# A windowed attention and MLP kernel: masks in three operations, the first loads in two portions, and a new hand-written order of all engines

## The chip, the cores and the metric

The kernel runs on one core of one Trainium2 chip. The metric is device time in microseconds (us) of one execution. The core has five engines that run their own instruction streams and meet only at semaphores: TensorE (PE in the profile; PEld is its weight load), VectorE (DVE), ScalarE (ACT), GpSimd (POOL) and SyncE (SP), which here issues nearly all DMA transfers.

## The reference, cut to what matters

There are 4 batches, 8 heads, 768 positions and a head size of 64. A query sees the `n_local` = 96 positions up to itself and the first `n_global` = 8 positions of the sequence; both numbers arrive as inputs. The bias falls with the distance, by a slope for each head. Behind attention stands an MLP from 512 to 2048 and back, on all 3072 rows.

```python
rel = pos[:, None] - pos[None, :]
is_global = pos[None, :] < int(n_global)
is_local = (rel >= 0) & (rel < int(n_local))
keep = is_global | is_local
dist = np.where(is_global & ~is_local, float(n_local), np.abs(rel))
scores = np.where(keep, scale * q @ k.T - slopes[:, None, None] * dist, -1e9)
a = softmax(scores); x = (a @ v).reshape(B * S, H * D)
h = x @ w_in                                   # 512 -> 2048
out = (h * tanh(log1p(exp(h)))) @ w_out        # 2048 -> 512
```

## The kernel before, in words

The work is cut into 12 chunks of 256 query rows (`NC`), three to a batch. A chunk has 16 attention pairs of a head and a 128-row block, taken in 8 tiles of two heads each; a tile sees its own 128 keys and, but for a sequence's first block, 104 more (96 before it and 8 global ones), so its score block is 128 or 232 columns wide. The MLP of a chunk has 8 steps of two 128-wide slices of the hidden layer.

`windowed` (L115) holds one small function for each step and, at its end, the table `PROGRAM`. Each word of the table is one call: a letter for the function (the dictionary `acts`) and a number for the tile, load, weight block or step; a stroke behind it (`L1'`) gives a copy to DVE instead of ACT, or a subtraction to DVE instead of POOL. Under `manual_schedule` every engine runs its instructions in just this order, and so do the transfers in SP's queue. Nothing reorders them: a wait on one engine holds back all that stands behind it there.

The words that matter here, with the lines of the profile:

- `e` (`begin`, L305): matmuls on a tile of ones (L313) whose result nothing reads; they only keep PE at work.
- `I`, `K0`, `K1` (L263 to L281): on DVE, the identity and the distances `d0` (own 128 columns) and `rel` (all 232), with a huge value where a key is not seen. They need `n`, which is loaded as 64-bit words and put together by L69 to L71. `L` and `M` scale them into the bias of each head, `mb0` and `mb` (a copy, L150 on DVE and L152 on ACT).
- `s` (`scores`, L426): for two tiles, the matmuls of q and k. `t` (`largest`, L440): on DVE, scores plus bias, and the row maximum. `y` (`exps`, L449): the exponentials on ACT. `P` (`turn_p`, L479): transposes on PE, `F` copies them out of PSUM (L150 or L152). `W` (`weigh`, L502 or L507): the product with v.
- The first three chunks (`CF32`) run in 32-bit matmuls straight on what was loaded; the others split every operand into two 16-bit halves.
- `q`, `v`, `x`, `w` (`load_qk` L165, `load_v`, `window_v`, `load_w` L325): loads. One `w` block is 512 KB. The weights come as 64-bit floats and are converted by `A`, `S`, `B` (`bits_w`, L364), `C` (L368), `D`, `E`.
- `i` (`moe_in`, L570) and `o` (`moe_out`, L626): the two matmuls of an MLP step; `j u n r` (ACT) and `G H` (DVE) are the activation between them, `z Z` its split into two halves.
- `Q` (`evacuate`, L628) and `Y` (`store`): results out of PSUM, and to memory. For the last chunk, `evacuate` takes each 128-row tile in two halves of 256 columns, the first on ACT (L635), the second on DVE (L636), and one store on SP follows (L642).
- `f` (`flags`, L646): four one-element operations on DVE that test `n`; only the last check needs them.

Of the kernel before, what the change touches and what calls it, by code (L numbers as in the profile page):

```python
# [42 lines left out]
def tile_kernel(ctx, tc, qd, kd, qT, kT, v, n, w_in, w_out, out):  # L43
# [71 lines left out]
def windowed(st, tc, loc):  # L115
# [49 lines left out]
    def load_qk(G):  # L165
        if G >= 2 * NC:
            return
        ci, g = divmod(G, 2)
        b, c = divmod(ci, NCHB)
        o = OWN if c == 0 else 0  # L170
        pairs = slice(g * GH // 2, (g + 1) * GH // 2)
        qr = raws.tile([P, GH // 2, CH], F32, name="qr", bufs=3)
        kr = raws.tile([P, GH // 2, KW], F32, name="kr", bufs=3)
        nc.sync.dma_start(qr, L.qT[b].rearrange("(a j) d s -> (j d) a s", j=2)[:, pairs, c * CH:(c + 1) * CH])
        for j in range(2):
            half = slice(j * D, (j + 1) * D)
            (nc.scalar if G == 0 and j else nc.sync).dma_start(kr[half, :, o:], L.kd[ci, half].rearrange("p (a j) w -> p a j w", j=2)[:, pairs, j, o:])
        raw[G] = (qr, kr)
# [71 lines left out]
    FAR = 2.0 ** 39  # L250
    jj = mt.tile([P, P], F32, name="u", bufs=3)
# [365 lines left out]
    def moe_out(m):  # L617
        ci, fp = divmod(m, NFP)
        if fp == 0:
            pos[ci] = [ps.tile([P, DM], F32, name=f"{'pav' if ci == 1 else 'po'}{t}", bufs=1) for t in range(2)]  # L620
        gt = gts.pop(m)
        for t in range(2):
            for j in range(2):
                fb = 2 * fp + j
                for n, (x, y) in enumerate(((0, 0), (0, 1), (1, 0))):
                    nc.tensor.matmul(pos[ci][t], gt[:, x, j, t * P:(t + 1) * P], wv4[:, 2 * fb + 1, y, :], start=(fb == 0 and n == 0), stop=(fb == NFB - 1 and n == 2))  # L626
# [19 lines left out]
    def flags():  # L646
        nc.vector.tensor_scalar(fl[:, 0:1], L.n_f[0:1, 0:1], 0.0, None, op0=ALU.is_ge)
# [15 lines left out]
    def checks(i):  # L663
# [40 lines left out]
        R2 H0 P17 s18 O2 W15 W14 y16 A4 F17 z0 t19 y19 C7 t18 T2' U2 E3 E1 Z0 P16 s20 P19 C4 t20 B6 t21 y18 F19 y20 F16' D4' E4' S5' A5 B12 R3 B5 o0 P20 P18
        s22 y21 F20 S12 A12 W17 O3 S6 T3 F18 A6 A8 C5 D7' t22 U3 W19 W20 P21 i8 E7 B8 C6 C12 t23 S8' D6' y22 F21 y23 j8 D5 E6 G8 E5' C8 B13 B10 S13' W21 P23
        W18 W16 P22 F22' R4 F23 u8 n8 S10 D12 r8 A13 D8 W23 i1 i9 w16 w11 E12 E8 H8 j1 A10 u1 S9 z8' C13 G1 j9 O4 W22 A14' Z8' C10 D10' R5 o8 u9 n1 n9 r1 r9
        T4 A15 S14 A11 E10 G9 A9' D13' E13 H1 U4 B14 i2 i10 z1 B9 C14 B15 B11 H9 Z1 S11 j2 z9 C11 C9 G2 h3' Z9' j10 u10 n10 D9 D11 r10 D14 u2 n2 S15' G10
        E9' S16' C15 H10 z10' r2 D15 A16 E14 w18 w24 w22 w21 w20 w17 w25 q6 w19 w26 Z10 H2 E11' o1 o9 i3 o10 O5 B16 S18 C16 A18 z2 j3 E15 Z2 u3 A17 n3 T5
        S17 A20 S20' r3 D16' G3 A24 B18 B17 U5 E16' B20 C18 B24 C17 D17 H3 o2 i11 i16 j11 z3 S24 G11 D18' E18 i12 w28 q7 w23 u11 J16 A22 n11 r11 Z3 C20 D20
        j12 A25' B19 E17 H11 S22' G12 A19 z11 C24 Z11' o3 i4 i17 D24 B22 E24 C22 E20 S19 u12 j4 D22 u4 n4 c7 n12 G4 S25' C19 B25 a7' C25 d7' b7 o11 s24 i18  # L710
        D19 r12 J17 r4 E22' H4 N0 t24 D25' A26' H12 t25 z4' J18 y25 A21 z12 E25' l3 E19' Z12' S26' B21 B26 Z4' i13 s26 i5 o12 j13 y24 G13 u13 S21 j5 A28 o4
        i20 q9 w30 w27 S28' C21 C26 D26' E26' B23 B28 t26 A30 u5 n5 D21 C28 g25 r5 n13 B30 G5 J20' S30' g24 E21' y26 r13 A23 H5 S23' i19 i6 p25' z5 A27 C23
        J19' D23 E23' c8' C30 H13 j6 u6 D28 g26 z13 B27 p26' Z5 Z13' D30' G6 E28' E30 p24 d8 w29 X25 w31 v4 X24 q8 x3 X26 i14 o5 i21 j14 u14 n6 r6 n14 S27
        r14 G14 H6 t27 S31 a8 i7 C27 y27 J21 z6 j7 u7 D27 B29 b8 S29' E27 Z6' H14 z14 Z14 i15 s28 o13 o14 o6 n7 r7 j15 u15 a9 n15 A31' A29' B31 G7 H7 t28
        C29 C31 G15 D31' z7' Z7' r15 D29 j16 u16 j17 y28 u17 n17 n16 r16 g27 H15 g28' p28' G16 z15' t29 E29 E31 H16 Z15 z16' G17 p27' Z16' o7 s30 o15 j18
        u18 y29 Q0 r17 q10 X28 Y0 o16 t30 g29' b9 H17 z17' Z17' h4' a11' t31 p29 y30 n18 r18 j19 u19 c9 G18 H18 d9' G19 z18' Z18 n19 Q1 r19 H19 j21 j20 o17
        W24 W25 i22 W26 W28 s32 o18 X29 X27 u21 z19 n21 r21 u20 g30 y31 n20 g31 p30 l4 c10' Z19' G21 t32 G20 t33 H21 p31' v5 x4 X30 X31 o19 W29 i23 W27 s34
        W30 W31 y32 z21 j22 u22 r20 y33 j23 a10 u23 n23 r23 n22 r22 R6 T6' H20 z20' U6 Z21 Z20 G22 g32' R7 T7' U7 H22 b10 z22 Z22' t35 y35 g33 p32' g35'
        d10' c11' d11 p33 G23 H23 t34 p35' o20 o21 V6 V7 o22 i24 s36 i25 Y1 X32 X33 X35 q11 t37 z23' j24 y34 u24 n24 y37 Z23' G24 j25 r24 H24 G25 t36 u25
# [196 lines left out]
```

## Time and profile before

| what | value |
|---|---|
| median of 3 runs | 621.35 us (617.2 to 621.35) |
| the profiled execution's own time | 624.25 us |
| its span, first to last instruction | 622.5 us |
| mean granted TensorE clock | 0.987 |
| PE busy | 610.3 us (98%) |
| DVE busy | 458.1 us (74%) |
| ACT busy | 441.3 us (71%) |
| POOL busy | 157.4 us (25%) |

The profile page cuts the span into 40 slices of 15.6 us; the row PEclk gives TensorE's granted clock in tenths of full speed. The view by windows gives the busy time of each engine in a stretch, the granted clock, the busy share of the DMA engines and what they moved. The timeline gives single instructions with their start, their duration, and in brackets how long the engine had been idle before and what ended that. The chain of waits follows what ended last back to its cause. A busy PE is not yet a PE at its peak, since the ends of matmuls are modelled.

### The profile page before, as it was taken

The numbers are of one execution on the slowest core, as the hardware profiler recorded it, in microseconds if no ns is written. First come the engines' busy times: TensorE is split into PE (matmuls) and PEld (weight loads), VectorE is DVE, ScalarE is ACT, GpSimd is POOL, SyncE is SP. The second block draws the span as 40 slices with busy tenths as digits, with TensorE's granted clock in tenths as the row PEclk, the third lists the DMA queues.
The fourth block names the chain that finished last, engine by engine and source line by source line (L and its number), as shares of the span: only waits on it lengthen the run. The fifth ranks groups of instructions, "written<-read, shape, count | busy, mean of one in ns | idle before, by whom it ended". The sixth has DMA issues, their size and how long they took to land.

```text
span 622.5 us, 13595 instructions
## 1 busy us (share of the span) xinstructions
PE 610.3 (98%) x5081; PEld 423.0 (68%) x5081; DVE 458.1 (74%) x1204; ACT 441.3 (71%) x1106; POOL 157.4 (25%) x130
## 2 busy tenths in 40 slices
PE   7999999999999999999999999999999999999996
PEld 3888867776466767676776676766667766766662
DVE  6599999989998779867676777776785766462443
ACT  5699887779895767766876758866865865665651
POOL 0031343104232250223233203223123332301020
PEclk9699999999999999999999999999999999999999
DMA  8994484235165739317256555392275434310001
GB/s 210 282 294 159 136 271 133 59 126 128 43 139 138 150 72 226 76 26 169 47 116 160 109 134 102 67 200 44 68 165 86 59 68 107 85 35 1 35 1 37
DMA packets 122358, 71.06 MB, mean 114 GB/s; under 512 B 91536, under 2 KB 112016, under 8 KB 122288
## 3 DMA queue, kind: packets, MB, share of 16 engines
q1 hardware_dynamic: 122144, 70.01, 47.3%
q8 instruction: 41, 0.67, 0.5%
q14 instruction: 29, 0.24, 0.1%
q10 hardware_dynamic: 144, 0.14, 0.1%
HBM read 38.62 MB, written 6.29 MB: 72 GB/s over the span
## 4 chain that ended last, share of the span: by engine, by line
PE 83%; DVE 9%; issue 3%; ACT 2%; DMA 1%; SPq 0%; POOL 0%; DVEq 0%; POOLq 0%
PE ph L570 35%; PE po L626 33%; PE sc L426 5%; PE pav L507 4%; PE pav L502 3%; DVE gf L608 2%; PE po L479 1%; DMA wts<-w_in 1%; DVE gf L604 1%; DVE ws L368 1%; PE pav L626 1%; DVE ws L364 1%; DVE gt L156 1%; DVE gt L150 0%; DVE A L440 0%
## 5 line engine op out<-in xcount | busy, mean ns | idle before, releaser
L570 PE MATMUL ph<-xT,wts 128*128 128x256 f16 x2304 | 263.6, 273 | 0.2 <-POOL wts L156 0.2
L570 PEld LDWEIGHTS <-wts 128*128 128x128 f16 x2304 | 222.8, 98 | 35.3 <-issue 1.7
L626 PE MATMUL po<-wts,gt 128*128 128x512 f16 x1056 | 238.7, 379 | 1.1 <-DVE gt L150 0.7
L626 PEld LDWEIGHTS <-gt 128*128 128x128 f16 x1152 | 110.0, 98 | 127.1 <-issue 2.8
L156 POOL TENSOR_TENSOR gt<-gf,gt 128x512 f16<-128x512 f32 x55 | 67.3, 1224 | 278.5 <-DVE gt L150 148.5
L588 ACT ACTIVATE e<-ph 128x512 f32<-128x512 f32 x90 | 53.1, 590 | 92.1 <-PE ph L570 91.8
L608 DVE CUSTOM_DVE_ANT_0 gf<-gf,u 128x512 f32<-128x512 f32 x96 | 79.7, 830 | 44.1 <-ACT u L600 43.1
L449 ACT ACTIVATE A<-A,nm 128x232 f32<-128x232 f32 (+1 forms) x192 | 88.4, 462 | 30.5 <-DVE nm L440 30.5
L604 DVE SCALAR_TENSOR_TENSOR gf<-e,ph 128x512 f32<-128x512 f32 x90 | 61.1, 682 | 53.2 <-ACT e L588 51.9
L440 DVE CUSTOM_DVE_ANT_0 A<-sc,mb 128x232 f32<-128x232 f32 (+1 forms) x192 | 64.3, 375 | 19.3 <-PE sc L426 16.7
L156 POOL TENSOR_TENSOR hl<-A,hl 128x512 f16<-128x512 f32 (+1 forms) x36 | 44.6, 1246 | 74.8 <-DVE hl L150 31.3
L592 ACT ACTIVATE u<-e 128x512 f32<-128x512 f32 x96 | 59.8, 624 | 1.8
L600 ACT ACTIVATE u<-u 128x512 f32<-128x512 f32 x96 | 59.4, 624 | 1.8
L596 ACT ACTIVATE u<-u 128x512 f32<-128x512 f32 x96 | 59.5, 623 | 1.6
L156 POOL TENSOR_TENSOR wts<-ws,wts 128x512 f16<-128x512 f32 x20 | 26.0, 1304 | 87.1 <-ACT wts L152 53.1
L152 ACT ACTIVATE gt<-gf 128x512 f16<-128x512 f32 x44 | 27.4, 623 | 21.3 <-DVE gmax L608 20.6
L449 ACT ACTIVATION_READ_ACCUMULATOR A<-A,nm 128x1 f32 x192 | 36.2, 188 | 0.0
L507 PEld LDWEIGHTS <-AT 128*128 128x128 f16 (+1 forms) x792 | 29.2, 97 | 6.3 <-issue 1.5
L156 DVE TENSOR_TENSOR hl<-A,hl 128x512 f16<-128x512 f32 (+1 forms) x36 | 29.9, 832 | 2.1 <-ACT hl L152 1.7
L156 DVE TENSOR_TENSOR gt<-gf,gt 128x512 f16<-128x512 f32 x41 | 29.0, 706 | 3.3 <-ACT gt L152 2.9
L507 PE MATMUL pav<-vo,AT 128*128 128x64 f16 x432 | 27.8, 192 | 0.0
L426 PE MATMUL sc<-wc,ws 64*128 64x232 f16 (+1 forms) x432 | 26.4, 254 | 0.3 <-DVE nm L440 0.2
(126 smaller groups left out, 608.5 us busy)
## 6 DMA issues: line engine op xcount, KB each, us to landing
qr<-qT SPq DMA_DIRECT2D x24, 256.0 KB
wts<-w_in SPq DMA_DIRECT2D x12, 512.0 KB
wts<-w_out SPq DMA_DIRECT2D x12, 512.0 KB
kr<-kd SPq DMA_DIRECT2D x32, 184.0 KB
out<-ob SPq DMA_DIRECT2D x11, 512.0 KB
vr<-v SPq DMA_DIRECT2D x9, 512.0 KB
vc<-vo SPq DMA_DIRECT2D x15, 192.0 KB
wr<-w_in SPq DMA_DIRECT2D x4, 512.0 KB
```

The source lines that it names most:

```text
L156: (nc.vector if other else nc.gpsimd).tensor_tensor(out, in_, high, op=ALU.subtract)
L426: nc.tensor.matmul(sc[j][:, a2, 0:w], x[half, a2, rows_], y[half, a2, col0:col0 + w], start=(n == 0), stop=(n == len(terms) - 1))
L440: nc.vector.tensor_tensor_reduce(out=A[:, j, 0:w], in0=sc[j][:, 0:w], in1=m, scale=-1.0 / (UNIT if ci < CF32 else UNIT * SQ), scalar=3.0e3 ...
L449: nc.scalar.activation(A[:, j], A[:, j], AF.Exp, bias=nm[:, h:h + 1], scale=-1.0, accum_out=rs[:, h:h + 1])
L507: nc.tensor.matmul(pav[:, cols], AT[rows_, (x * 2 + j) * nk + kk, :], vs[kk][rows_, y, cols], start=(n == 0), stop=(n == last))
L570: nc.tensor.matmul(ph[:, j, :].rearrange("p (b t) -> p b t", b=2), wv4[:, 2 * fb, x, c * P:(c + 1) * P], xT[:, :, y * NCC + c, :], start=( ...
L592: nc.scalar.activation(u, mish[m]["e"], AF.Square, bias=0.5)
L596: nc.scalar.activation(mish[m]["r"], mish[m]["u"], AF.Ln, bias=0.25 / RS, scale=1.0 / RS)
L600: nc.scalar.activation(r, r, AF.Exp, scale=-1.0)
L604: nc.vector.scalar_tensor_tensor(gf, mish[m]["e"], 0.5, mish[m]["h"], op0=ALU.add, op1=ALU.mult)
L608: nc.vector.tensor_tensor_reduce(out=gf, in0=gf, in1=mish[m]["r"], scale=SG / (SV * SW * RS), scalar=0.0, op0=ALU.mult, op1=ALU.max, accum ...
L626: nc.tensor.matmul(pos[ci][t], gt[:, x, j, t * P:(t + 1) * P], wv4[:, 2 * fb + 1, y, :], start=(fb == 0 and n == 0), stop=(fb == NFB - 1 a ...
```

## The change

It does six things.

1. `n` is no longer put together from its two words before the masks: they use the low word (`n_w`), and the three small operations move to `flags`.
2. The masks of the own block take three operations after `n` (L267 once, L272, L273) in place of five; what does not need `n` stands in `identity`, ahead of it.
3. The first q and k loads are cut into two portions, first the 128 columns that the first score block needs; one of the first k portions is issued by ACT, the rest by SP.
4. The matmuls on ones are 10, 4 and 1 in place of 13 and 2, and stand in other places.
5. In the last MLP step the last tile's matmuls run in two halves of 256 columns; the first half is copied by DVE and stored through SP, the last half is copied by ACT and stored by ACT itself.
6. `PROGRAM` is another order up to its last 160 words; many strokes changed too.

```diff
-    two32 = 4294967296.0
     wv = n_w.rearrange("p (n w) -> p n w", w=2)
-    nc.vector.tensor_scalar(n_neg, wv[:, :, 0], 0.0, two32, op0=ALU.is_lt, op1=ALU.mult)
-    nc.vector.tensor_tensor(n_neg, n_neg, wv[:, :, 0], op=ALU.add)
-    nc.vector.scalar_tensor_tensor(n_f, wv[:, :, 1], two32, n_neg, op0=ALU.mult, op1=ALU.add)
...
+        if G == 0:
+            for cq, ck in ((slice(0, P), slice(o, o + P)), (slice(P, CH), slice(o + P, KW))):
+                nc.sync.dma_start(qr[:, :, cq], qs[:, :, cq])
+                for j in range(2):
+                    (nc.scalar if j == 0 and ck.start == o else nc.sync).dma_start(kr[halves_[j], :, ck], ks[j][:, :, ck])
+        else:
+            nc.sync.dma_start(qr, qs)
...
     def identity(i):
         nc.vector.tensor_scalar(idn, rel[:, own], 0.0, None, op0=ALU.is_equal)
+        nc.vector.tensor_scalar(off[:, own], rel[:, own], 0.0, NEVER, op0=ALU.is_lt, op1=ALU.mult)
+        nc.vector.tensor_tensor(rel[:, own], rel[:, own], off[:, own], op=ALU.add)
 
     def outside(cols):
-        nc.vector.tensor_scalar(off[:, cols], rel[:, cols], 0.0, None, op0=ALU.is_lt)
-        nc.vector.scalar_tensor_tensor(off[:, cols], rel[:, cols], L.nlf, off[:, cols], op0=ALU.is_ge, op1=ALU.max)
+        nc.vector.tensor_scalar(off[:, cols], rel[:, cols], nl, FAR, op0=ALU.is_ge, op1=ALU.mult)
 
     def masks_own():
         outside(own)
-        nc.vector.scalar_tensor_tensor(k0, jj, L.ngf, off[:, own], op0=ALU.is_ge, op1=ALU.mult)
-        nc.vector.scalar_tensor_tensor(d0, rel[:, own], L.nlf, off[:, own], op0=ALU.subtract, op1=ALU.mult)
-        nc.vector.tensor_tensor(d0, rel[:, own], d0, op=ALU.subtract)
-        nc.vector.scalar_tensor_tensor(d0, k0, FAR, d0, op0=ALU.mult, op1=ALU.max)
+        nc.vector.scalar_tensor_tensor(k0, jj, ng, off[:, own], op0=ALU.is_ge, op1=ALU.mult)
+        nc.vector.scalar_tensor_tensor(d0, rel[:, own], nl, k0, op0=ALU.min, op1=ALU.max)
...
         for t in range(2):
-            for j in range(2):
...
+            for cols in parts(m, t):
+                for j in range(2):
+                    fb = 2 * fp + j
+                    for n, (x, y) in enumerate(((0, 0), (0, 1), (1, 0))):
+                        nc.tensor.matmul(pos[ci][t][:, cols], gt[:, x, j, t * P:(t + 1) * P], wv4[:, 2 * fb + 1, y, cols], ...)
+    def parts(m, t):
+        if m < NC * NFP - 1 or t == 0:
+            return (slice(0, DM),)
+        return slice(0, DM // 2), slice(DM // 2, DM)
...
-                half = DM // 2
-                nc.scalar.activation(ob[:, t, 0:half], po[t][:, 0:half], AF.Copy, scale=1.0 / (SG * SW))
-                nc.vector.tensor_scalar(ob[:, t, half:], po[t][:, half:], 1.0 / (SG * SW), None, op0=ALU.mult)
-                store(ci, slice(t, t + 1))
+                for cols in parts(NC * NFP - 1, t):
+                    early, final = t and cols.start == 0, t and cols.stop == DM
+                    copy(ob[:, t, cols], po[t][:, cols], 1.0 / (SG * SW), early)
+                    (nc.scalar if final else nc.sync).dma_start(L.out[n * P:(n + 1) * P, cols], ob[:, t, cols])
...
     PROGRAM = """
-        e13 I0 K0 L2 K1 L4 L0 L3 v0 w2 q1 x0 s0 e2 t1 y1 M3 P1 L1' t0 s2 B2 F1' f0 M0 M2 M1 L5 y0 A2 t3 t2 P0 W1 y3 P3 q2 w0 v1 w1 q3 x1 s4 ...
+        e10 I0 v0 q1 K0 K1 L4' L2 x0 s0 e4 L0' L1' L5' L3 M1 t0 t1 y0 L6 M2 q2 s2 y1 L7' M0' M3' P0 t3 w0 P1 F1' F0 y3 w2 e1 W0 t2 M6' W1 y2 P3 f0 s4 ...
```

What the table does to SP's queue at the start (`n_i` is n, `qr` and `kr` are q and k, `vo` is v, `wts` a weight block): before it read

```order
L62 DMA n_i<-n 128x4
L174 DMA qr<-qT 128x2x256
L177 DMA kr<-kd 64x2x264
L211 DMA vo<-v 128x2x512
L333 DMA wts<-w_in 128x4x256
L174 DMA qr<-qT 128x2x256
L177 DMA kr<-kd 64x2x264 x2
```

and now

```order
L62 DMA n_i<-n 128x4
L175 DMA qr<-qT 128x2x128
L177 DMA kr<-kd 64x2x128
L175 DMA qr<-qT 128x2x128
L177 DMA kr<-kd 64x2x136 x2
L215 DMA vo<-v 128x2x512
L179 DMA qr<-qT 128x2x256
L181 DMA kr<-kd 64x2x264 x2
```

The weight block no longer stands ahead of the second group's q and k; the first group's load has become five entries here instead of two.

On DVE, between the maxima of the first two tiles and those of the next two (`A,nm<-sc,mb` 128x232; `ws` and `fl` are a weight conversion and the flags, `AT` a transposed tile), the order was

```order
L440 ISA nm_171 128x1
L364 TENSOR_SCALAR ws<-wts 128x512
L150 TENSOR_SCALAR AT<-po_178 128x256
L647 TENSOR_SCALAR fl<-n_f 1x1
L648 TENSOR_SCALAR fl<-n_f,fl 1x1
L649 TENSOR_SCALAR fl<-n_f,fl 1x1
L650 TENSOR_SCALAR fl<-n_f,fl 1x1
L440 ISA A,nm_208<-sc,mb 128x232
```

and is now

```order
L445 ISA nm_170 128x1
L146 TENSOR_SCALAR mb_95<-u 128x128
L146 TENSOR_SCALAR mb<-e 128x232 x2
L445 ISA A,nm_201<-sc,mb 128x232
L445 ISA nm_201 128x1
L445 ISA A,nm_201<-sc,mb 128x232
```

The weight conversion, which waits for its load, and the flags have left this place; three bias copies have come in.

## Rows read from the trace of the kernel before

**Rows 1.** The profile page: the span, and TensorE's granted clock in 40 slices.

```profile
span 622.5 us, 13595 instructions
...
PEclk9699999999999999999999999999999999999999
```

**Rows 2.** Windows: stretch, its length, busy us by engine (instructions), clock, DMA share, GB/s.

```profile
4.00:6.00 2.00, 2.00 (x7) 0.71 (x6) 1.72 (x7) 0.00 (x0) 0.00 (x0) 1.00 1.04 269
...
8.00:10.00 2.00, 1.64 (x10) 0.96 (x10) 0.46 (x5) 2.00 (x10) 0.00 (x0) 1.00 1.13 293
...
12.00:14.00 2.00, 1.14 (x6) 0.63 (x6) 2.00 (x13) 1.77 (x8) 0.00 (x0) 0.63 1.09 189
14.00:26.00 12.00, 12.00 (x58) 10.00 (x58) 5.60 (x24) 5.23 (x21) 0.00 (x0) 0.50 1.08 274
26.00:28.00 2.00, 2.00 (x19) 2.00 (x19) 1.94 (x11) 1.53 (x5) 0.00 (x0) 0.95 1.08 350
28.00:62.00 34.00, 34.00 (x286) 28.97 (x286) 31.71 (x111) 32.46 (x94) 7.38 (x6) 1.00 0.80 229
62.00:200.00 138.00, 135.77 (x1062) 93.67 (x1060) 129.57 (x281) 113.03 (x260) 41.05 (x31) 1.00 0.46 128
```

**Rows 3.** The chain of waits, first 30 us: start us, us, what.

```profile
3.10 7.23 DMA wts<-w_in
...
17.84 1.85 PE sc L426 x8
...
28.37 0.98 PE sc L426 x8
```

**Rows 4.** Timeline of DVE, 3 to 13 us: start, us, instruction, idle before it.

```profile
3.97 0.17 DVE L69 TENSOR_SCALAR n_neg<-n_w 128x2 f32<-128x2 f32 x1
...
4.57 0.35 DVE L268 SCALAR_TENSOR_TENSOR e<-e,n_f 128x128 f32<-128x128 f32 x1
...
7.40 0.28 DVE L440 CUSTOM_DVE_ANT_0 A<-sc,mb 128x128 f32<-128x128 f32 x1
...
7.82 0.22 DVE L150 TENSOR_SCALAR mb<-u 128x128 bf16<-128x128 f32 x1
...
10.35 0.46 DVE L364 TENSOR_SCALAR ws<-wts 128x512 uint16<-128x512 uint16 x1 [1.89 <-DMA wts<-w_in]
...
11.03 0.13 DVE L647 TENSOR_SCALAR fl<-n_f 1x1 f32<-1x1 f32 x1
...
11.80 0.39 DVE L440 CUSTOM_DVE_ANT_0 A<-sc,mb 128x232 f32<-128x232 f32 x1
```

**Rows 5.** Timeline of PE, and one load's issue on SP, 0 to 14 us.

```profile
1.58 5.00 PE L313 MATMUL ph<-ws 128*128 128x512 f16 x13 [1.58 <-DVE ws L309]
6.51 0.71 PE L426 MATMUL sc<-kr,qr 64*128 64x128 f32 x8
...
12.86 1.16 PE L479 MATMUL po<-idn,A 128*128 128x128 f32 x4 [1.04 <-ACT A L449]
13.96 0.58 PE L426 MATMUL sc<-kr,qr 64*128 64x128 f32 x2
...
1.67 0.76 SPq L177 DMA_DIRECT2D kr<-kd  x1
```

**Rows 6.** PE's waits after 26 us, first and last of five: us, times, longest.

```profile
PE po L626 <- DVE gt L150: 0.7, 1, 0.7
...
PE ph L570 <- POOL wts L156: 0.2, 1, 0.2
```

**Rows 7.** Timeline of the last copies and stores, and the one load that ACT issues.

```profile
615.90 1.72 SPq L642 DMA_DIRECT2D out<-ob  x2
616.33 0.38 ACT L635 ACTIVATE ob<-po 128x256 f32<-128x256 f32 x1 [0.91 <-PE po L626]
616.75 0.42 DVE L636 TENSOR_SCALAR ob<-po 128x256 f32<-128x256 f32 x1 [0.87 <-ACT ob L635]
...
0.83 0.74 ACTq L177 DMA_DIRECT2D kr<-kd  x1
```

More of the change, by code (lines that the diff above doesn't have):

```diff
@@ L173, in load_qk @@
         kr = raws.tile([P, GH // 2, KW], F32, name="kr", bufs=3)
-        nc.sync.dma_start(qr, L.qT[b].rearrange("(a j) d s -> (j d) a s", j=2)[:, pairs, c * CH:(c + 1) * CH])
-        for j in range(2):
-            half = slice(j * D, (j + 1) * D)
-            (nc.scalar if G == 0 and j else nc.sync).dma_start(kr[half, :, o:], L.kd[ci, half].rearrange("p (a j) w -> p a j w", j=2)[:, pairs, j, o:])
+        qs = L.qT[b].rearrange("(a j) d s -> (j d) a s", j=2)[:, pairs, c * CH:(c + 1) * CH]
+        ks = [L.kd[ci, j * D:(j + 1) * D].rearrange("p (a j) w -> p a j w", j=2)[:, pairs, j] for j in range(2)]
+        halves_ = [slice(j * D, (j + 1) * D) for j in range(2)]
+        if G == 0:
[6 more added lines that the diff above has]
+            for j in range(2):
+                nc.sync.dma_start(kr[halves_[j], :, o:], ks[j][:, :, o:])
         raw[G] = (qr, kr)
@@ L250, in windowed @@
     FAR = 2.0 ** 39
+    NEVER = 2.0 ** 20
+    ng, nl = L.n_w[:, 0:1], L.n_w[:, 2:3]
     jj = mt.tile([P, P], F32, name="u", bufs=3)
@@ L622, in moe_out @@
         for t in range(2):
[L623 to L626, printed above, removed]
+            for cols in parts(m, t):
+                for j in range(2):
+                    fb = 2 * fp + j
+                    for n, (x, y) in enumerate(((0, 0), (0, 1), (1, 0))):
+                        nc.tensor.matmul(pos[ci][t][:, cols], gt[:, x, j, t * P:(t + 1) * P], wv4[:, 2 * fb + 1, y, cols], start=(fb == 0 and n == 0), stop=(fb == NFB - 1 and n == 2 and cols.stop == DM))
+    def parts(m, t):
+        if m < NC * NFP - 1 or t == 0:
+            return (slice(0, DM),)
+        return slice(0, DM // 2), slice(DM // 2, DM)
     def evacuate(ci):
@@ L646, in flags @@
     def flags():
+        two32 = 4294967296.0
+        nc.vector.tensor_scalar(L.n_neg, L.wv[:, :, 0], 0.0, two32, op0=ALU.is_lt, op1=ALU.mult)
+        nc.vector.tensor_tensor(L.n_neg, L.n_neg, L.wv[:, :, 0], op=ALU.add)
+        nc.vector.scalar_tensor_tensor(L.n_f, L.wv[:, :, 1], two32, L.n_neg, op0=ALU.mult, op1=ALU.add)
         nc.vector.tensor_scalar(fl[:, 0:1], L.n_f[0:1, 0:1], 0.0, None, op0=ALU.is_ge)
@@ L704, in windowed @@
[L704 to L719, printed above, removed]
@@ L752, in windowed @@
[L752 to L755 removed]
+        e10 I0 v0 q1 K0 K1 L4' L2 x0 s0 e4 L0' L1' L5' L3 M1 t0 t1 y0 L6 M2 q2 s2 y1 L7' M0' M3' P0 t3 w0 P1 F1' F0 y3 w2 e1 W0 t2 M6' W1 y2 P3 f0 s4 F3 q3
@@ L756, in windowed @@
+        H87 z87 Z87 i89 o86 j89 j88 u88 G88 n88 o87 r88 u89 H88 n89 z88' Z88' r89 Q10 G89 i90 H89 Y10 z89' Z89 o88 j90 u90 G90 n90 r90 i91 H90 o89 j91 u91
+        G91 n91 r91 i92 H91 z91' z90' Z91 Z90 i93 j92 G92 o90 j93 u92 n92 r92 u93 o91 H92 n93 G93 r93 k0 z92' Z92' H93 i94 z93' Z93 i95 j94 u94 G94 n94 r94
+        o92 H94 j95 u95 G95 n95 z94 r95 o93 Z94 H95 z95 o94 k1 Z95' o95 k2 Q11
     """
```

98 lines of the change are left out of this document (55 added, 43 removed).

## The prediction, made before the changed kernel ran

> **What bounds the kernel now.** I read the page first. PE is the engine that is nearly always busy, and its granted clock is full in all slices but the first two [rows 1]. So a change of order can win only where PE waits, where it runs slowly, and behind its last matmul. The windows show where that is. From 28 us on PE is busy in all of a stretch at clock 1.00, or nearly: 34.00 of 34.00, then 135.77 of 138.00 [rows 2]. Its waits after 26 us come to five, 2.0 us in all, 0.7 the longest [rows 6]. What is left lies in the first 26 us. PE is busy 1.64 of 2 us in 8 to 10 and 1.14 of 2 in 12 to 14; then the clock is 0.63 for a slice, 0.50 from 14 to 26, and 0.95 in the slice after [rows 2]. The 0.63 and the 0.95 put the fall at 12.5 us and the return at 26.2: a stretch of 13.7 us on the lower of the two levels, 1.2 in place of 2.4 GHz. The same eight score matmuls took 1.85 us in it and 0.98 after it [rows 3].
>
> Why PE had gaps before the clock fell, the chain of waits says. It passes through one weight load: issued at 3.10, on the way for 7.23 us [rows 3]. DVE stood still for the last 1.89 us of that, at 10.35, since a weight conversion was its next instruction [rows 4]. Behind it stood a copy that PE's product waits for, the flags from 11.03, and at 11.80 the maxima of the second tile pair. ACT's exponentials and PE's transposes at 12.86, after 1.04 us without work, follow from these [rows 4, 5].
>
> **The head start.** Up to the second group's scores, at 13.96 us [rows 5], I follow the new order through the same durations.
>
> - Masks: DVE's run from L69 at 3.97 to the first maximum at 7.40 is 13 operations [rows 4]. Now there are seven after `n`, but four bias copies of 0.22 have come ahead of that maximum. Six operations fewer at 0.17 to 0.35, so some 1.5 us, less about 0.8 for the copies, is 0.7 us earlier.
> - Ones: 13 took 5.00 us [rows 5]; three fewer are 1.15 us at that mean, so the first scores, at 6.51, can start some 0.7 to 1.1 us earlier. Four ones now stand behind them. The two gains run side by side and count once.
> - Second pair: its maxima started at 11.80. In the new order they stand right behind the first pair's and three bias copies (0.7 us), so at about 8.4: the wait of 1.89, the conversion of 0.46 and the four flags (11.03 to 11.80) are gone from here. PE's transposes come about 3 us earlier with them.
> - Data for the second group: in the old queue the weight block was the last of some 1.54 MB (first q and k 0.52, v 0.51, weights 0.51), and was there at 10.33, where the chain has its end [rows 3]. Now v and the second group's q and k end at 1.55 MB, so at about the same time if the queue stays as full (269 to 293 GB/s, share over 1.0 [rows 2]). PE can then start these scores near 10.7 to 11, which is 3.0 us earlier. This, not DVE, is what is late next.
>
> The split itself I price by issue time: three more entries in SP's queue at up to 0.76 us each [rows 5] are 2.3 us at most, if none of it hides behind transfers that are still under way. The share is already 1.04 from 4 to 6 us [rows 2], so transfers are under way behind which some of it hides. I take **3.0 us**, with 0.7 and 3.5 as ends.
>
> A rule speaks against the portions. The Trainium skill, "DMA: Bandwidth & Descriptors", section "Measured (HBM→SBUF, 128 partitions, SWDGE, issued from GpSimd)", asks for transfers of 1 MiB or more and gives 138 GB/s for 64 KB. By it the first 0.52 MB would take 3.8 us and the sum would lose about 1.9 us. In this trace loads of 0.13 to 0.51 MB follow each other in one queue at 269 GB/s [rows 2], so I leave it at the end of the range.
>
> **The clock.** In the new order PE's gaps from 8 to 13 us mostly close: the transposes and scores move up, and four ones and one more fill two of the places where it waited. A PE that had 1.64 and 1.14 of 2 us before the fall, and kept its clock with 2.00 of 2 ever after [rows 2], should then keep it here. What stood in the 12.2 us from 14 to 26.2 takes 6.1 us at full clock, if the others follow. In 14 to 26 DVE was busy 5.60 and ACT 5.23 us [rows 2]. Squeezed to 6.1 us that is 92 and 86%; both engines show 93 and 95% from 28 to 62 (31.71 and 32.46 of 34) [rows 2], so it is possible, and tight. I take **6.0 us**; 0 if the clock falls as before.
>
> **Is it kept?** After 26 us the new order has the same PE work in almost the same sequence. POOL, ACT and DVE trade operations by their strokes. DVE is the one to watch: 129.57 of 138 us busy from 62 to 200 [rows 2]. If PE is 9 us ahead, DVE fills its 6.4 idle us of 14 to 26 and still has 2.3 idle in 28 to 62 and 8.4 in 62 to 200, 17.1 in all, of which 9 go: some 8 stay, as many as it has from 62 to 200 now, where PE lost 2.2 us [rows 2]. I cost the new order after 26 us at **0**, from -2.0 (all the waits of [rows 6] gone) to +2.2 (as many again as 62 to 200 has).
>
> **The end.** Before, PE's last matmul was followed by ACT's half (0.38), then DVE's (0.42), then a store on SP [rows 7]. Now only ACT's half stands there and ACT issues the store. The copy on DVE and the step to it are gone, 0.45 us, and the last store is half as large. Against it stands ACT's issue, which took 0.74 us the one time it is seen [rows 7], longer than SP's last ones can have taken if that is the price here too. Twelve matmuls of 256 columns in place of six of 512 cost nothing that I can see. I take **0.5 us**, from 0 to 1.
>
> **Sum.** 3.0 + 6.0 + 0 + 0.5 = 9.5 us off the profiled execution's 624.25, so 614.75 (its span 622.5 to 613.0). The median of the runs is 2.9 below the profiled one: 611.85. I say **612 us**.
>
> **Rivals.**
>
> *The clock falls all the same* (0.20). The second group's data may come a microsecond later, and where in the run the clock is judged cannot be chosen; the lowest run of before, 617.2 against twice 621.35, may be one in which less of the stretch was lost. For it: the new margin hangs on single loads. Against it: ones now lie in the gaps. With a stretch as long as before the sum is 3.5, so 617.9; with half of it, 614.9. The Trainium skill, "TensorE: Matmul & The Clock Gate", section "What's actually happening", says that the number of slow matmuls at the start changes from run to run of one kernel, and holds the loss to be under 1% of a typical span; the 13.7 us here cost half of that, 6.8, which is 1.1%.
>
> *DVE becomes the bound* (0.08). The clock holds, but from 62 to 200 us DVE's idle time does not lie where it is needed, and PE waits for half of what it had gained: 4.5 us given back, 616.4. For it speaks the 94% of DVE there [rows 2]; against it that DVE has eight idle us left.
>
> *The loads become the bound, and the kernel slower* (0.06). The DMA engines are at 1.08 from 14 to 28 us [rows 2], and the new queue puts weights behind q, k and v that wait for buffers which PE must first free. If the first MLP step's weights are late, PE stands, and the clock falls there: the 9.0 us are lost and a stretch as long as the old one costs its 6.1 us again, 621.35 - 0.5 + 6.1 = 627. It decides from the point where a weight block lands later than its conversion is due by more than the head start. Against it: no load but that one weight block held DVE after the start, and none held PE.
>
> That the change does nothing at all would need the ones, the portions and the moved weight block to fail together; I give it no chance of its own.
>
> **Chances.** 0.66 for the forecast, 0.20, 0.08, 0.06 for the others. About 1%, 6.2 us, is what a measurement of this kernel can tell from no change; faster by that means below 615.1. The forecast lies there but for its upper edge, and a third of the clock's rival does: 0.66. Slower by over 1% is above 627.6, the upper half of the loads' rival: 0.04. The same: 0.30. The forecast's own range, against the median, is 608.9 (head start 3.5, 2.0 of waits gone, 1.0 at the end) to 616.4 (head start 0.7, 2.2 more of waits). To leave out no more than 2 in 10 it must reach to the clock's rival at 617.9: **608.5 to 618**.
>
> **What would show it.** In the changed profile: DVE's first conversion of a weight (L369) behind the maxima of several tiles, without a wait of 1.9 us ahead of those; the second group's scores near 11 us; PEclk at 1.00 in the windows from 12 to 26; PE at 2.00 of 2 us there with DVE and ACT over 85%; no store behind a DVE copy at the end. A clock of 0.5 in any window from 10 to 30 us makes the second term wrong, PE waits over 2 us in all after 26 the third, and scores of the second group after 12.5 us the first.

## The result, and the profile after

The changed kernel took **614.28 us** (median of 5 runs, 613.29 to 614.58), the kernel before beside it 621.35 us (617.2 to 622.34): a ratio of 0.9893, 95% interval 0.9858 to 0.9928. The forecast was 612.0. Between the two profiled executions the difference is 624.25 - 614.36 = 9.9 us; the sum of the prediction was 9.5.

The runs of before differ by their clock: of 68 runs of the kernel before that later comparisons used, 47 had a mean granted clock of 0.997 or more and took 617.6 us in the median, the other 21 had 0.987 to 0.994 and took 620.2 to 624.5, while all 17 runs of the changed kernel had 0.997 or more (median 614.4). So the ratio depends on how many runs of before keep their clock: beside another 20 runs of it, 0.9932 (0.9909 to 0.9956). Five more runs of before, with clocks of 0.982 and 0.983, took 626.6 to 628.0 us and are not among the 68. Of the five runs of before beside the first measurement four took 621.35 us or more, so that its 1.1% owe something to chance: against runs of before with a full clock the change is worth 617.6 - 614.4 = 3.2 us, 0.5%.

The page of the changed kernel has the clock full in every slice; before it was low in the second [rows 1]. A slice is 15 us here.

```profile
span 612.5 us, 13603 instructions
...
PEclk9999999999999999999999999999999999999999
```

The windows, in the columns of [rows 2]:

```profile
4.00:6.00 2.00, 2.00 (x7) 0.49 (x5) 1.86 (x9) 0.71 (x3) 0.00 (x0) 1.00 0.63 138
...
8.00:10.00 2.00, 2.00 (x15) 1.15 (x13) 1.19 (x8) 1.95 (x10) 0.00 (x0) 1.00 1.11 287
...
12.00:14.00 2.00, 2.00 (x22) 1.81 (x21) 1.89 (x13) 1.80 (x8) 0.00 (x0) 1.00 1.06 248
14.00:26.00 12.00, 12.00 (x102) 10.22 (x102) 9.62 (x42) 10.54 (x37) 0.00 (x0) 1.00 1.07 309
26.00:28.00 2.00, 2.00 (x21) 2.00 (x20) 2.00 (x8) 2.00 (x7) 0.00 (x0) 1.00 1.09 208
28.00:62.00 34.00, 34.00 (x289) 29.14 (x289) 31.52 (x103) 30.78 (x83) 10.64 (x10) 1.00 0.97 300
62.00:200.00 138.00, 138.00 (x1084) 94.19 (x1083) 124.89 (x291) 120.57 (x275) 32.86 (x26) 1.00 0.48 124
```

Two more stretches, each before and now:

```profile
6.00:14.00 8.00, 5.86 (x35) 3.12 (x33) 5.93 (x34) 6.23 (x26) 0.00 (x0) 0.91 1.08 260
200.00:550.00 350.00, 350.00 (x3185) 241.04 (x3184) 251.50 (x663) 246.20 (x632) 98.66 (x78) 1.00 0.50 106
```

```profile
6.00:14.00 8.00, 8.00 (x60) 5.86 (x61) 6.00 (x39) 6.38 (x27) 0.00 (x0) 1.00 1.06 277
200.00:550.00 350.00, 347.94 (x3152) 239.52 (x3151) 241.61 (x645) 247.84 (x629) 96.20 (x78) 1.00 0.52 102
```

From 6 to 200 us PE is busy in all of every stretch. In 14 to 26 its count went from 58 matmuls to 102 at clock 1.00, with DVE at 9.62 of 12 and ACT at 10.54: 80 and 88%, where the prediction asked for over 85 of both. From 62 to 200 the 2.23 us that PE lacked are there, and DVE does 124.89 us of work where it did 129.57. New are 2.06 us without PE from 200 to 550. PE's waits name them; the second row is its start, as before:

```profile
PE pav L512 <- DMA AT<-hl: 2.1, 2, 1.3
PE ph L318 <- DVE ws L314: 1.6, 1, 1.6
```

The five waits of [rows 6] are gone. In their place PE twice waits, at 391 and at 532 us, for a tile of attention weights (`AT`) that a DMA transposes.

The timeline of DVE, answering to [rows 4]: the first mask, the first maximum, that of the second pair, and the first of the operations on `n`.

```profile
3.66 0.28 DVE L275 TENSOR_SCALAR e<-e,n_w 128x128 f32<-128x128 f32 x1
...
7.23 0.29 DVE L445 CUSTOM_DVE_ANT_0 A<-sc,mb 128x128 f32<-128x128 f32 x1 [0.98 <-PE sc L431]
...
9.48 0.40 DVE L445 CUSTOM_DVE_ANT_0 A<-sc,mb 128x232 f32<-128x232 f32 x1 [0.81 <-PE sc L431]
...
11.29 0.16 DVE L660 TENSOR_SCALAR n_neg<-n_w 128x2 f32<-128x2 f32 x1
```

No maximum waits for a weight any more, and both wait for PE's scores, 0.98 and 0.81 us. The first conversion (L369) comes at 16.32 us, without a wait.

The timeline of PE, answering to [rows 5]:

```profile
1.59 4.45 PE L318 MATMUL ph<-ws 128*128 128x512 f16 x10 [1.59 <-DVE ws L314]
5.96 1.23 PE L431 MATMUL sc<-kr,qr 64*128 64x128 f32 x8
7.13 1.23 PE L318 MATMUL ph<-ws 128*128 128x512 f16 x4
8.29 1.05 PE L431 MATMUL sc<-kr,qr 64*128 64x232 f32 x8
...
11.66 0.82 PE L431 MATMUL sc<-kr,qr 64*128 64x128 f32 x8
```

The second group's scores moved from 13.96 to 11.66. The first eight took 1.23 us, before 0.71 [rows 5]: in this run the trace records the clock at full from 7.55 us on, before from 5.71. When it first rises differs from run to run (4.5 to 7.6 us in the profiles of this case). As an estimate, it costs or gives about half of the shift. That is worth keeping in mind below, where differences are under 1 us.

The end, answering to [rows 7]:

```profile
604.17 2.78 PE L632 MATMUL po<-wts,gt 128*128 128x512 f16 x18
...
606.29 1.74 SPq L649 DMA_DIRECT2D out<-ob  x2
606.98 0.42 DVE L146 TENSOR_SCALAR ob<-po 128x256 f32<-128x256 f32 x1 [1.08 <-PE po L632]
607.44 0.38 ACT L148 ACTIVATE ob<-po 128x256 f32<-128x256 f32 x1 [1.17 <-DVE ob L146]
607.86 0.36 ACTq L649 DMA_DIRECT2D out<-ob  x1
```

PE ends at 606.95. Only then does DVE copy the half whose matmuls ended earlier, and only behind that ACT the other. From PE's end to the end of the span it is 5.52 us, before 6.17. One profile each cannot carry this difference: of the experiments below, e3 and e4 keep the old end and take 5.99 and 5.43 us for it, while the profiles with the new end take 5.25 to 5.96.

### The profile page after: what moved, and what is told of

It reads as the page before. It is cut to its first block, busy times and chain, and to the rows that moved or that the text cites. A ratio compares the mean times of both kernels' runs of the same rounds, so it can differ in the third digit from the quotient of the medians.

```text
span 612.5 us, 13603 instructions
## 1 busy us (share of the span) xinstructions
PE 603.3 (99%) x5087; PEld 419.4 (68%) x5087; DVE 440.8 (72%) x1193; ACT 450.2 (74%) x1117; POOL 148.6 (24%) x127
## 4 chain that ended last, share of the span: by engine, by line
PE 97%; DMA 1%; DVE 0%; issue 0%; ACT 0%; DVEq 0%; SPq 0%
PE ph L575 41%; PE po L632 37%; PE sc L431 6%; PE pav L512 4%; PE pav L632 3%; PE pav L507 3%; DMA AT<-hl 1%; PE po L484 1%; PE ph L318 1%; PE ph L484 1%; PE ph L530 0%; PE sc L690 0%; DVE ws L314 0%; DVE ob L146 0%; ACT ob L148 0%
## 5 line engine op out<-in xcount | busy, mean ns | idle before, releaser
L632 PE MATMUL po<-wts,gt 128*128 128x512 f16 (+1 forms) x1062 | 239.0, 378 | 0.0
L613 DVE CUSTOM_DVE_ANT_0 gf<-gf,u 128x512 f32<-128x512 f32 x96 | 73.9, 773 | 49.8 <-ACT u L605 47.9
L152 POOL TENSOR_TENSOR gt<-gf,gt 128x512 f16<-128x512 f32 x43 | 52.3, 1218 | 221.3 <-DVE gt L146 150.9
L152 POOL TENSOR_TENSOR hl<-A,hl 128x512 f16<-128x512 f32 (+1 forms) x44 | 50.8, 1164 | 114.2 <-ACT hl L148 56.3
L152 DVE TENSOR_TENSOR gt<-gf,gt 128x512 f16<-128x512 f32 x53 | 39.0, 737 | 5.3 <-ACT gt L148 4.5
L512 PEld LDWEIGHTS <-AT 128*128 128x128 f16 (+1 forms) x792 | 29.4, 97 | 9.8 <-DMA AT<-hl 2.8
L148 ACT ACTIVATE gt<-gf 128x512 f16<-128x512 f32 x34 | 21.2, 623 | 11.7 <-DVE gmax L613 10.8
L146 DVE TENSOR_SCALAR gt<-gf 128x512 f16<-128x512 f32 x62 | 27.6, 450 | 1.4
L148 ACT ACTIVATE hl<-A 128x512 f16<-128x512 f32 (+1 forms) x43 | 25.3, 591 | 2.6 <-DMA AT<-hl 2.1
```

The source lines that it names most:

```text
L152: (nc.vector if other else nc.gpsimd).tensor_tensor(out, in_, high, op=ALU.subtract)
L512: nc.tensor.matmul(pav[:, cols], AT[rows_, (x * 2 + j) * nk + kk, :], vs[kk][rows_, y, cols], start=(n == 0), stop=(n == last))
L613: nc.vector.tensor_tensor_reduce(out=gf, in0=gf, in1=mish[m]["r"], scale=SG / (SV * SW * RS), scalar=0.0, op0=ALU.mult, op1=ALU.max, accum ...
L632: nc.tensor.matmul(pos[ci][t][:, cols], gt[:, x, j, t * P:(t + 1) * P], wv4[:, 2 * fb + 1, y, cols], start=(fb == 0 and n == 0), stop=(fb ...
```

## The experiments

Each of the twelve was compared with runs of the kernel before on the same chip. The median of these was 618.26 us beside e1 to e4, 617.61 beside e5 to e8 and 618.14 beside e9 to e12.

### The start and the rest, exchanged

**e1_new_start** has the changed kernel's code and order up to `s12`, then before's order; **e2_new_rest** the reverse.

```diff
# e1: words of the new table up to s12, then those left, in the old order
# e2: words of the old table up to s12, then those left, in the new order
```

> The changed kernel with its own order up to the scores of the fourth group (s12, in its trace near 20 us) and the old order for all that is left. If the gain is made in the first 26 us (head start and clock) and only kept later, this runs in 613 to 616 us with the clock at 1.00 from 12 to 26 us. If the new order of the later steps makes it, 619 to 622.

Measured: **625.6 us** (625.1 to 626.56), ratio 1.0095 (1.0064 to 1.0127): slower than before, and than either branch of the expectation. The timeline, the windows (28:62 and the two ahead of it) and PE's longest wait in e1:

```profile
28.21 0.46 DVE L369 TENSOR_SCALAR ws<-wts 128x512 uint16<-128x512 uint16 x1 [3.94 <-DMA wts<-w_out]
28.21 0.68 ACT L148 ACTIVATE wc<-wts 128x512 f32<-128x512 f32 x1 [4.10 <-DMA wts<-w_out]
```

```profile
14.00:26.00 12.00, 9.80 (x83) 8.28 (x81) 7.23 (x33) 9.29 (x30) 0.00 (x0) 1.00 1.07 312
26.00:28.00 2.00, 0.00 (x0) 0.00 (x0) 0.00 (x0) 0.00 (x0) 0.00 (x0) 1.00 1.11 216
28.00:62.00 34.00, 32.08 (x215) 26.19 (x216) 27.75 (x91) 26.54 (x73) 6.98 (x6) 0.80 0.74 226
```

```profile
PE po L484 <- ACT A L454: 5.6, 1, 5.6
```

The new start loads weights later; the old rest converts them as early as ever. DVE and ACT both stood for a `w_out` block, PE stood 5.6 us behind them, from 23.8 to 29.4, and the clock fell at 28.4. This is the prediction's third rival, the loads as the bound, with its price: 627 forecast, 625.6 measured. It did not come true in the changed kernel, whose later part asks for the weights later as well.

> The reverse: the old order up to s12 with its early weight block and its ones, then the new order; masks, portions and the new end stay. If the start makes the gain, the conversion of the weight block holds DVE again near 10 us, the clock falls near 12 us, and the time is 619 to 622 us. If the later order makes it, 613 to 616.

Measured: 620.89 us (618.77 to 626.83), ratio 1.004 (1.0003 to 1.0078). All ten runs had a clock of 0.981 to 0.995. The window of e2:

```profile
14.00:26.00 12.00, 12.00 (x80) 10.31 (x80) 7.83 (x37) 7.29 (x29) 0.00 (x0) 0.72 1.07 307
```

With the old start the clock falls, here in every run, while in the kernel before it does so in 21 of 68; why it does so more often here is open. Masks, portions and the new end do not keep it; the order of the start does, as e5 will show again with the old order behind it.

### What keeps the clock

**e3_ones_only** is the kernel before with seven more matmuls on ones in two places where PE stood; **e4_weight_later** the kernel before with the one early weight block moved behind.

```diff
- ... y0 A2 t3 t2 P0 W1 y3 P3 q2 ...
+ ... y0 A2 t3 t2 e2 P0 W1 y3 e5 P3 q2 ...                     # e3
- ... L3 v0 w2 q1 ... s2 B2 F1' ... y0 A2 t3 ... q2 w0 ... s6 P4
+ ... L3 v0 q1 ... s2 F1' ... y0 t3 ... q2 w2 w0 ... s6 B2 A2 P4   # e4
```

> The kernel before with seven more matmuls on ones in the places where PE waited between 10 and 13 us, nothing else. If the granted clock is what costs most of the start, it stays at 1.00 through 14 to 26 us and the time falls by 4.5 to 6.5 us, to about 615.5, without any head start. If the clock only follows from the late data and DVE and ACT would set the pace anyway, the clock is 1.00 and the time still 620 to 622.

> The kernel before with the first weight block loaded behind the third group's q and k and its first conversions behind the scores s6, nothing else. If the early block was what held the start, the second group's scores come 2 to 3 us earlier than 13.96 and, the gaps of PE being shorter, the clock mostly stays: 614.5 to 618 us. If masks, ones and portions were needed for it, the scores come at 13 us or later, the clock falls, and the time is 620 to 622.

Measured: e3 619.14 us (618.39 to 621.42), ratio 0.9998 (0.9971 to 1.0026); e4 617.29 (616.48 to 617.72), ratio 0.9956 (0.9926 to 0.9987). All ten runs of each had a clock of 0.997 or more. The two windows in question in e3, then in e4:

```profile
12.00:14.00 2.00, 1.97 (x16) 1.02 (x13) 2.00 (x13) 2.00 (x9) 0.00 (x0) 1.00 1.09 229
14.00:26.00 12.00, 11.97 (x101) 10.25 (x99) 10.38 (x47) 10.07 (x38) 0.00 (x0) 1.00 1.08 266
```

```profile
12.00:14.00 2.00, 2.00 (x19) 1.63 (x19) 2.00 (x12) 0.74 (x4) 0.00 (x0) 1.00 1.09 296
14.00:26.00 12.00, 11.67 (x100) 9.99 (x99) 10.21 (x43) 11.50 (x40) 0.00 (x0) 1.00 1.07 302
```

Either alone keeps the clock; of the 24 runs of before that stand beside them, 16 had it. Where the clock fell, PE had 1.14 busy us of 2 in 12 to 14 [rows 2]; e3 has 1.97 there and e4 2.00.

The time of e3 is not the forecast 615.5: it lies 1.6 us above the 617.6 that the kernel before needs when its clock stays full. The seven ones take some 1.5 us (five of them 1.24), but they stand in part where PE was idle before, and in the profile of e3 PE also stands still for 1.54 us later on, where in the kernel before it never does:

```profile
200.00:550.00 350.00, 348.46 (x3153) 239.70 (x3150) 250.35 (x660) 244.97 (x628) 98.72 (x78) 1.00 0.51 104
```

So what the ones cost by themselves stays open. e4 lands 0.3 us below the 617.6. Its second group's scores in the timeline of PE:

```profile
12.02 0.71 PE L426 MATMUL sc<-kr,qr 64*128 64x128 f32 x8
```

They start 1.9 us earlier than in the profile of before, just short of the 2 to 3 that the expectation of e4 asked for, and yet there is hardly a gain beyond the clock. So the clock is nearly the whole of what moving the weight block gives, and the kernel before has it already in 47 runs of 68.

What the changed kernel gains beyond that, 617.6 - 614.4 = 3.2 us, must come from elsewhere. The profiles of e4 and of the changed kernel, both at full clock, have spans of 615.0 and 612.5 us. In the changed kernel PE is idle 1.55 us less from 6 to 26 us, 2.26 less from 62 to 200 and 2.06 more from 200 to 550; it is also busy 0.9 us less (603.3 for 604.2), which is not traced, and its end takes 0.1 us more.

### The later order

**e5_old_late** takes the new order up to `o8`, some 60 us in, and the old from there, so that the weights of e1 are not in question.

```diff
# words of the new table up to o8, then those left, in the old order
```

> The changed kernel with its new order as far as o8 (some 60 us into the span, when every weight block of the first chunk is in place) and from there the order of before. If the later order is worth the waits of TensorE that are gone between 62 and 200 us (2.2 us of idle TensorE in the kernel before, none in the changed one): 616.5 us (615.8 to 617.3), with TensorE idle about 2 us in 62 to 200 again. If the later order is worth nothing, as my prediction put it: 614.3 us, the time of the changed kernel.

Measured: **616.11 us** (614.75 to 617.54), ratio 0.9956 (0.9932 to 0.9979); 1.7 above the changed kernel. Its windows:

```profile
62.00:200.00 138.00, 135.67 (x1075) 92.39 (x1073) 129.05 (x286) 115.14 (x265) 37.08 (x29) 1.00 0.46 122
200.00:550.00 350.00, 349.66 (x3152) 239.83 (x3150) 251.57 (x661) 245.15 (x627) 98.16 (x78) 1.00 0.50 104
```

The 2.3 us of idle PE are back in 62 to 200, and the waits of 200 to 550 shrink from 2.06 to 0.34. By the times the later order is worth 1.7 us, about half of the 3.2. The waits alone do not make that up: where the two orders differ, e5 has 2.33 + 0.34 us without PE and the changed kernel 2.06, so 0.6 more; the rest is not traced.

**e9_turns** asks what the two new waits cost: the steps that waited come behind one more MLP step.

```diff
- ... v10 W69 o57 W68 ...          - ... r81 W92 H81 W93 R22 i82 z81' ...
+ ... v10 o57 W69 W68 ...          + ... r81 H81 i82 W92 W93 z81' R22 ...
```

> The changed kernel with two steps of TensorE's order exchanged: the weigh steps that stood still for transposed tiles at 391 and 532 us (0.9 and 1.5 us) come behind one more step of the second network product (o57, i82). If these waits are all that these steps cost: 2.1 us less, 612.2 us (611.7 to 613.0), and TensorE busy 350.0 of 350 in 200 to 550 us. If what is moved makes another step late (the rows step of the last chunk, W69's tile): 613.5 to 615 us.

Measured: **611.77 us** (611.51 to 612.57), ratio 0.9886 (0.9852 to 0.992), beside 614.45 for the changed kernel (e12). Its window:

```profile
200.00:550.00 350.00, 350.00 (x3170) 241.52 (x3169) 241.37 (x646) 248.84 (x631) 96.18 (x78) 1.00 0.51 102
```

The waits were nothing but a matter of order, and nothing else became late. It is the best version of this study. Of the 2.7 us, 2.06 are these waits; the rest I can't assign.

### Masks, portions, ones, end

**e10_old_masks** handles `n` and makes the masks as before, in the new order (the diff of those functions, turned around).

> The changed kernel with n handled and masks made as before (three operations on n first, seven more on the masks), in the new order. In the changed kernel the first maximum waits 0.98 us for TensorE's scores, so the masks are not what it waits for. If that wait covers the masks of before: 614.3 us (614.0 to 614.8). If the three operations and the longer masks (some 1.5 us of DVE) are on the path: first maxima 0.5 to 1.5 us later, TensorE idle for as much before 14 us, 615 to 616 us.

Measured: 614.5 us (614.3 to 615.33), ratio 0.992 (0.9889 to 0.9952), against 614.45. DVE's first maximum and PE's second scores in e10:

```profile
7.66 0.28 DVE L450 CUSTOM_DVE_ANT_0 A<-sc,mb 128x128 f32<-128x128 f32 x1
```

```profile
8.43 1.26 PE L436 MATMUL sc<-kr,qr 64*128 64x232 f32 x8 [0.87 <-DVE nm L450]
```

The first maximum comes 0.43 us later than in the first profile of the changed kernel and 0.69 later than in that of e12 (6.97), and no longer waits for PE; PE waits 0.87 us instead. The time does not show it. In the profile the clock is recorded at full from 5.73 us, 0.80 sooner than in e12, which as an estimate hides about half of that. Between nothing and 0.9 us the shorter masks' worth stays open.

**e7_whole_qk** loads the first q and k whole.

```diff
-            for cq, ck in ((slice(0, P), slice(o, o + P)), (slice(P, CH), slice(o + P, KW))):
+            for cq, ck in ((slice(0, CH), slice(o, KW)),):
```

> The changed kernel with q and k of the first group loaded whole, as before, not in two portions of 128 columns. If the first scores wait for these loads: they start some 0.5 us later, the second group's scores follow by as much, 614.9 us (614.3 to 615.6). If the loads run beside the ones and the masks: no difference, 614.3 us.

Measured: 613.73 us (613.32 to 614.48), ratio 0.9921 (0.9894 to 0.9948). The same two rows of PE as in the changed kernel, and its window of 4 to 6 us:

```profile
5.96 0.96 PE L431 MATMUL sc<-kr,qr 64*128 64x128 f32 x8
...
11.32 0.71 PE L431 MATMUL sc<-kr,qr 64*128 64x128 f32 x8
```

```profile
4.00:6.00 2.00, 2.00 (x6) 0.48 (x4) 1.81 (x10) 0.62 (x3) 0.00 (x0) 1.00 0.98 238
```

The first scores start at 5.96 either way, behind the ones; the portions bring nothing. They do fill the DMA engines less, 138 GB/s against 238 in this stretch. The Trainium skill, "DMA: Bandwidth & Descriptors", section "Measured (HBM→SBUF, 128 partitions, SWDGE, issued from GpSimd)", gives 138 GB/s for 64 KB, and by it the prediction estimated a loss of 1.9 us. The loss did not come: PE waited for no load. That the stretch has the same rate is chance, for it is the mean of uneven parts (175 GB/s from 4 to 5 us, 51 from 5.8 to 6).

**e6_first_ones** leaves out the five later matmuls on ones (`e4`, `e1` in the table); **e11_both** does so on top of e9.

```diff
- ... x0 s0 e4 L0' ... y3 w2 e1 W0 ...
+ ... x0 s0 L0' ... y3 w2 W0 ...
```

> The changed kernel with only the ten matmuls on ones at the start; the four ahead of the last transposes of the first group and the one ahead of weigh are left out (five matmuls that compute nothing). If the clock is held by the kernel's own work, which now comes without a gap from the second group on: 614.3 us (613.5 to 615.0), clock full to the end. If these ones hold it: the clock falls, or rises later, somewhere in the first 30 us, and the time is 617 us or more.

> e9_turns and e6_first_ones in one kernel: the two exchanged steps, and without the five later matmuls on ones. If the two savings add (1.7 us and 2.1 us): 610.5 us (610.0 to 611.5). If the ones are needed once the rest is earlier: the clock falls in some runs, 613 us or more.

Measured: e6 612.62 us (612.02 to 612.91), ratio 0.9895 (0.9854 to 0.9936); e11 612.23 (611.24 to 613.14), ratio 0.9888 (0.9854 to 0.9923). No run's clock was below 0.997: these ones do not hold it. Both times miss their forecasts, e6 below its 613.5 to 615.0, e11 above its 610.0 to 611.5. On the saving the two disagree: in e6 it is some 1.7 us, in e11 nothing beside e9. PE in e11, and two of its waits:

```profile
7.88 1.26 PE L431 MATMUL sc<-kr,qr 64*128 64x232 f32 x8 [0.81 <-DVE nm L445]
```

```profile
PE sc L431 <- DVE nm L445: 0.8, 1, 0.8
PE pav L512 <- DMA AT<-hl: 0.5, 1, 0.5
```

Without the four ones PE stands 0.81 us for the maxima that free the score banks, so most of their 1.2 us come back as a wait, and a transposed tile is late again by 0.5. The same stall is in e6; but there the transposes' waits happened to be 0.9 in place of 2.1 us, and the clock was full from 5.58 us. So most of e6's gain need not be the ones'. What they cost by themselves stays open.

**e8_split_end** gives the second half of the last 128 rows a PSUM bank and an SBUF tile of its own. For this its matmuls run in halves through the whole last chunk, 42 more of them; by the profiles these cost 0.1 us.

```diff
+            if ci == NC - 1:
+                pos[ci].append(ps.tile([P, DM], F32, name="pav1", bufs=1))
...
-        if m < NC * NFP - 1 or t == 0:
+        if m < (NC - 1) * NFP or t == 0:
...
-    nc.tensor.matmul(pos[ci][t][:, cols], ...
+    nc.tensor.matmul(pos[ci][t if cols.start == 0 else 2][:, cols], ...
...
+                    src, dst = (po[2], ob2[:, cols]) if final else (po[t], ob[:, t, cols])
```

> The changed kernel with the second half of the last 128 rows in a PSUM bank and an SBUF tile of its own through the whole last chunk, so that the copy of its first half can start before the last matmul has ended. If DVE's copy and ACT's copy stand one behind the other at the end because they share a tile, and not because of their engines: one copy less behind the last matmul, 0.45 us less, 613.8 us (613.5 to 614.2); between the last matmul and the end of the span 5.1 us instead of 5.55. If the store's flight alone sets the end: 614.3 us.

Measured: 614.43 us (613.79 to 616.32), ratio 0.9935 (0.991 to 0.996). The end in e8, whose span is 614.3:

```profile
607.85 0.82 PE L634 MATMUL pav<-wts,gt 128*128 128x256 f16 x6
608.02 0.83 SPq L653 DMA_DIRECT2D out<-ob  x2
608.05 0.42 DVE L146 TENSOR_SCALAR ob<-po 128x256 f32<-128x256 f32 x1 [0.42 <-PE po L634]
608.77 0.38 ACT L148 ACTIVATE gf<-pav 128x256 f32<-128x256 f32 x1 [0.77 <-PE pav L634]
609.18 0.36 ACTq L653 DMA_DIRECT2D out<-gf  x1
```

The mechanism worked: DVE copies while PE still runs, and ACT starts 0.10 us behind the last matmul, not 0.49. It gained nothing; the 613.8 us forecast for it (613.5 to 614.2) did not come, and the end is 5.61 us behind PE's last matmul, where it was 5.52. The copies are closer together now, and so are the stores: issued at 608.02, 608.51 and 609.18, in the changed kernel at 606.29, 607.68 and 607.86. The busiest half microsecond behind them, first in the changed kernel, then in e8:

```profile
608.50:609.00 0.50, 0.00 (x0) 0.00 (x0) 0.00 (x0) 0.00 (x0) 0.00 (x0) 1.00 0.85 289
```

```profile
609.50:610.00 0.50, 0.00 (x0) 0.00 (x0) 0.00 (x0) 0.00 (x0) 0.00 (x0) 1.00 1.07 322
```

The DMA engines' share is 1.07 in place of 0.85, and ACT's store takes 3.4 us to land, not 2.9; in the ten profiles whose stores stand as in the changed kernel it takes 2.7 to 3.1. So what the copies gave, the store took. That it queues behind the others is the likely reason, not one that a run shows by itself.

**e12_changed_again** is the changed kernel beside e9 to e11.

> The changed kernel itself again, beside the others of this call. Every theory: 614.3 us (613.3 to 614.9), and the kernel before some runs near 617.4 us with the clock full throughout and some 620 to 628 us with a stretch at half clock, while the changed kernel has none with such a stretch.

Measured: 614.45 us (613.59 to 617.65), ratio 0.9932 (0.9909 to 0.9956). One run, at a clock of 1.000, took 617.65 us, 2.2 more than any other, so not all of the spread is the clock's.

## Why the prediction was right, step by step

PE's account closes the difference of the spans, 622.5 - 612.5 = 10.0 us: it was idle 3.0 us less (2.14 in 6 to 14 us, 2.23 in 62 to 200 and 0.65 at the end, less 2.06 more in 200 to 550) and busy 7.0 us less (the pages have 610.3 and 603.3).

- **The head start: 3.0 forecast, 2.3 measured** at the second group's scores, within its ends of 0.7 and 3.5. What it is worth in time is not shown by itself: e4 had 1.9 of it and gained 0.3 beyond the clock. The parts were less good. The second pair's maxima came at 9.48, not 8.4: PE's scores ahead of them stood behind four ones and began at the lower clock (in e12, with the clock full 1.0 us sooner, they came at 9.03). And data were not what is late next: in e6 these scores started at 11.15, so the loads were there by then, and in the changed kernel PE had no idle time ahead of them; it was its own work in order. Portions and masks, which I had priced at up to 2.3 us of loss and 0.7 of gain, move the time by less than these comparisons resolve (e7, e10).
- **The clock: 6.0 forecast.** The lower clock of 13.7 us, worth 6.8, is gone; a rise 1.8 us later at the start took back up to 0.9. The rest of the 7.0 us, about 1, I have not traced. That there was a term to win is luck of the profiled execution, which was one of those that lose their clock; in 47 of 68 runs of before it is 0. The link to PE's gaps is shown from both sides: where ones or a later weight block take away most of PE's gap of 1.04 us ahead of the fall, the clock stays (e3, e4), though earlier gaps of up to 0.7 us are still there; with the old start it falls (e2), and with a new gap of 5.6 us it falls in that gap (e1). What decides between the runs of before, no run shows.
- **The order after 26 us: 0 forecast, 0.2 measured**, but of two parts: 2.2 us of waits gone in 62 to 200, the end of my range on that side, and 2.1 new ones in 200 to 550. That they cancel is luck, and by my own sign, waits of over 2 us after 26, the term fails by a hair. I had given DVE's spare time as the limit. DVE was relieved by 4.7 us there, and the new waits were the transposing DMA's, on which I had no row.
- **The end: 0.5 forecast, 0.65 measured, by another way.** I wrote that the copy on DVE was gone from behind the last matmul. It is still there, and ACT's behind it; what shrank is the store, 2.9 us from issue to landing in place of 3.8. With the old end e4 has 3.05 us for it and as short an end as the changed kernel, so that a gain of this size is likely but not shown.
- **The step that failed is the last line of the sum.** From 614.75 for the profiled execution I took off the 2.9 us by which the median of before lay below its profiled run. That offset was itself the clock's stretch, longer in the profiled run (clock 0.987) than in the median one (in the later comparisons, runs of before near 621.35 us have 0.993), and my second term had removed it. It counted twice: 611.85 where 614.75 was meant, and 614.28 came.
- **The rivals.** The clock did not fall in any of the 17 runs. DVE did not become the bound. The loads did not in this kernel; with the old order behind the new start they did (e1).

## What to carry to other kernels

A term that the runs have only at times (here a stretch at half clock in 21 of 68) must be taken off the run that shows it, and the result stands for all runs; what the spread of the old kernel does to its median belongs to the old kernel alone. A new order is not a sum of pieces: moving loads later was safe where the work that waits for them was moved later too (e4), and the new start without the new rest made the kernel slower than before (e1). When a profile shows two waits for a DMA on an engine that is otherwise full, put one more independent step ahead of them: two exchanged words gave 2.7 us, nearly as much as the whole change gives where the clock holds.

## What was not expected of the hardware

- The granted clock first became full at times between 4.5 and 7.6 us, though PE ran the same ones from 1.59 us on in several of these profiles (7.55 in the changed kernel, 6.53 in the same kernel again, 5.58 in e6).
- The stretch at the lower clock is not there in most runs of the kernel before: its 68 runs fall into 616.8 to 619.9 us and 620.2 to 624.5. The Trainium skill, "TensorE: Matmul & The Clock Gate", section "What's actually happening", speaks of a varying number of slow matmuls at a kernel's start; here it is a fall at 12.5 us, and PE's idle time around it is 0.36 of 2 us in 8 to 10 and 0.86 in 12 to 14 [rows 2].
- Stores that leave within 1.2 us of each other (e8) went with a last store that took 0.5 us longer than with the same three within 1.6 us; starting the last copy earlier was worth nothing.
